# Batch 1's third split into fetch, rows and gate steps, with scaling and copies on ScalarE

## The chip, the cores and the metric

The kernel runs on one core of one Trainium2 chip. The metric is the device time of one execution in microseconds, lower is better. Engines are named as in the profile: PE is TensorE (PEld its weight loads), DVE is VectorE, ACT is ScalarE, POOL is GpSimd, SP is SyncE, which issues most DMA transfers. A queue's DMA issues are marked SPq, ACTq and POOLq.

## The reference

Three layers follow one another on 4 batches of 3072 tokens with 256 channels:

```
X  = rfft(x, axis=1)                       # spectral layer
Y  = shrink(X @ (w_r + i w_i) + b, 0.01)   # real and imaginary part each
y  = irfft(Y)                              # 12288 tokens x 256
logits = y @ w_gate; e = argmax; gate = softmax(logits)[e]
disp[e, pos] = y[i] for the first 384 tokens of each of 8 experts
h  = relu(disp @ w1[e]) @ w2[e];  out[i] = gate[i] * h[e, pos]
g  = out @ w_in;  result = (g * sigmoid(g)) @ w_out
```

At most 8 x 384 tokens go through an expert; all other rows of the result are zero.

## The kernel before

Every matrix product in reduced precision is made of three matmuls over a high and a low part of both operands (`mm3`, lines 208 to 210). High parts are cast by ACT (`hi`, line 192), low parts are differences made by DVE or POOL (`lo`, line 200). The order of instructions on each engine is set by a scheduler when the program is built: it takes the program in the order in which the generators are stepped, keeps dependencies, and places each instruction by a model of time. `after` adds an order for this scheduler only; on the chip it is no wait. Each DMA signals one of eight semaphores in turn, and a DMA that takes a semaphore waits until the earlier DMA on it has landed.

`near` computes batch 0 and the spectra of batch 1 (written to `b_d`). Tokens of batch 0 are routed, and the first experts, sorted so that those that batch 0 fills come first, can begin. `experts` then runs the order 0, 1, 2, E, 3, 4, E+1, 5, 6, E+2, 7, E+3, where a number is an expert's first layer (`first_ffn`) and E the second one for a pair of experts (`second_ffn`).

`first_ffn` makes 8 blocks j: six matmuls into a PSUM tile `hp` (operands `xT` and `w` of line 1066's loads), a relu by ACT into `hh`, the low part `hl` by DVE, and six matmuls into two accumulators `y`. It yields 9 times. At the end the two accumulators are copied to `yf`, one by ACT (line 1130), one by DVE (line 1131); only then can the next expert write its own. `weights` loads an expert's weights in four quarters through four buffers `st` of 256 KB; each load waits until the split of an earlier one has read its buffer. `turn` scales the gathered rows `xg` of the next expert by their gate (line 1095, three pieces on DVE), transposes them on PE (`gtp`) and splits them into `xT`. `pair` makes the operands `ms` and `yT` of the second layer by sums of two experts' `yf`.

Beside experts 0 to 2 runs `third(1)`: the last part of batch 1's inverse transform for a third of its tokens, with their logits, in four steps n. `rows(n)` fetches 768 KB of `b_d` in two DMAs on SP's queue (tiles `br`, `bi`, `by`; line 587), makes eight matmuls (line 590), copies to `ao` (ACT) and writes `attn` in four DMAs; `gate(n)` transposes `ao` on PE (`tp`), copies to `aT` on DVE (line 606) and makes the logits (`lg`); every second one is followed by a transpose `lt` and by `choose`, a chain of small DVE operations with an Exp on ACT. `rows(n)` and `gate(n-1)` stand in one step. Then `route` turns choices into places: a scan, the sums `bs` on PE, a chain on DVE up to `pm`, eight matmuls `tb`, and `slots`.

`beside` yields the count at which it wants to be stepped next, in blocks j over all experts: 7, then 8, 10, 12, 14 and 16, so the steps fall into experts 0 and 1.

Of the kernel before, what the change touches and what calls it, by code (L numbers as in the profile page):

```python
# [9 lines left out]
F32 = mybir.dt.float32  # L10
FR = mybir.dt.float32r
I32 = mybir.dt.int32
ALU = mybir.AluOpType
AF = mybir.ActivationFunctionType
# [5 lines left out]
Q = 96  # L20
# [3 lines left out]
P = 128  # L24
LAM = 0.01
NT = B * S
QB, GT = 32, 8
# [13 lines left out]
RING = 2  # L41
LATE = 3
PACE = {4: 2, 5: 5, **{n: GT - 1 for n in range(6, 12)}}
HOLD = {10: "lt", 14: "bs", 18: "tb"}
BIG = 65536.0
UP = 65536.0
# [109 lines left out]
class Kernel:  # L156
# [202 lines left out]
    CH = 512  # L359
# [209 lines left out]
    def third(self, b, res):  # L569

        nc, bp, ps, wg, CH = self.nc, self.bp, self.ps, self.wg, self.CH
        v = nc.vector
        c4 = self.c4[:Q, 64:]
        bv = self.bds[b].rearrange("k (r u g) c -> (k r) u (g c)", r=4, u=4)
        od = self.attn[0][b * S:b * S + QB * TW].rearrange("(q u g) d -> u q (g d)", u=4, g=GT)
        res[b] = self.chosen(1)
        idle = self.mg.tile([P, 3, 2, CH], F32, tag="ms", name="bi", bufs=1)
        room = {n + 2: idle[:Q, n] for n in range(3)}
        room[5] = self.mh.tile([P, 2, CH], F32, tag="yT", name="by", bufs=1)[:Q]

        def rows(n):
            pt = ps.tile([P, CH], F32, tag="ps", name="ps2")
            for w in range(2):
                br = room.get(2 * n + w)
                if br is None:
                    br = bp.tile([Q, 2, CH], F32, tag="xt", name="br", bufs=self.sb)
                nc.sync.dma_start(out=br, in_=bv[:, 2 * w:2 * w + 2, n * CH:(n + 1) * CH])
                for z in range(2):
                    u = 2 * w + z
                    ins = nc.tensor.matmul(pt[u * QB:(u + 1) * QB], c4, br[:, z], start=True, stop=True).ins  # L590
                    if b == 1 and not u:
                        self.after(ins, self.lasty)
            ao = bp.tile([P, 2, 2, P], F32, tag="ao", name="ao2")
            aof = ao.rearrange("p g h d -> p (g h d)")
            nc.scalar.copy(aof, pt)
            for u in range(4):
                nc.sync.dma_start(out=od[u, :, n * CH:(n + 1) * CH], in_=aof[u * QB:(u + 1) * QB])
            return ao

        def gate(n, ao):  # L600
            tp = ps.tile([P, 2, 2, P], F32, tag="ps", name="tp")
            for g in range(2):
                for h in range(2):
                    nc.tensor.transpose(tp[:, g, h], ao[:, g, h], self.ident)
            aT = bp.tile([P, 2, 2, P], F32, tag="aT", name="aT", bufs=1)
            v.tensor_copy(aT, tp)
            if n % 2 == 0:
                self.lg = ps.tile([P, P], F32, tag="ps", name="lg")
            for h in range(2):
                for g in range(2):  # L610
                    at = COL * (2 * (n % 2) + g)
                    nc.tensor.matmul(self.lg[at:at + COL], wg[:, h], aT[:, g, h], start=h == 0, stop=h == 1)
            if n % 2:
                ls = bp.tile([P, P], F32, tag="ls", name="ls", bufs=1)
                nc.scalar.copy(ls, self.lg)
                lt = ps.tile([P, 4, COL], F32, tag="ps", name="lt")
                nc.tensor.transpose(lt.rearrange("p g e -> p (g e)"), ls, self.ident)
                self.choose(lt.rearrange("p (o g) e -> p o g e", o=1)[:, :, :, :E], res[b], slice(2 * n - 2, 2 * n + 2))

        ao = {}  # L620
        for n in range(GT // 2 + 1):
            if n < GT // 2:
                ao[n] = rows(n)
            if n:
                gate(n - 1, ao.pop(n - 1))
            yield

    def is2(self, b, qbs, res):
# [320 lines left out]
    def experts(self, again=False):  # L949
        tc = self.tc  # L950
        tag = "b" if again else "a"
# [6 lines left out]
        ps = dict(space=bass.MemoryType.PSUM)  # L958
# [10 lines left out]
        def beside():  # L969

            with self.stream("b", 2, "left"):
                yield 7
                for n, _ in enumerate(self.third(1, self.res)):
                    yield 8 + 2 * n
                tiny = self.mc.tile([P, 1], F32, name="tiny")
                self.route(1, (0,), self.res)
                self.sl.extend(self.slots(self.mc, EARLY, E, self.sel, "t")[0])
                self.after(self.nc.scalar.activation(tiny, self.zt[:, 0, :1], AF.Silu).ins, self.exps)
                self.filled()
                zeros()  # L980
            self.po, self.mb = pool("po", **ps), pool("mb")
# [22 lines left out]
        n = 0  # L1004
# [87 lines left out]
    def turn(self, rows, behind=None):  # L1092
        xg, gw = rows
        for j in range(SC):
            ins = self.nc.vector.tensor_scalar(xg[:, j], xg[:, j], gw[:, j:j + 1], None, ALU.mult)
            if behind:
                self.after(ins.ins, behind)
        xT = self.mx.tile([P, 2, 2, CAP], FR, tag="xT", name="xT")
# [7 lines left out]
    def first_ffn(self, e, xT, ws):  # L1106
# [21 lines left out]
            yield  # L1128
        y = self.ys[e] = self.mg.tile([P, 2, CAP], F32, tag="yf", name="yf", bufs=3)
        nc.scalar.copy(y[:, 0], yp[0])  # L1130
        nc.vector.tensor_copy(y[:, 1], yp[1])

    def pair(self, behind=None):

# [256 lines left out]
```

## Time and profile before

| what | us |
|---|---|
| median of 3 runs | 616.54 (615.39 to 617.16) |
| the profiled execution | 617.55 |
| its span, first to last instruction | 615.8 |
| PE busy in the span | 593.4 |
| DVE busy | 424.7 |
| ACT busy | 339.3 |
| POOL busy | 187.0 |

A span is the time between the first and the last instruction of the profiled execution; the execution's own time is 1.75 us longer. An engine's busy time says what it did, not what limited the kernel. Rows in order of time give the start, the length, the engine with the line of the program, the operation, the tile written and the tile read, the shape, a count, and in brackets the idle time before it with the instruction that ended it. The granted clock of TensorE is 1.00 at 2.4 GHz and 0.50 at 1.2 GHz.

### The profile page before, as it was taken

Reading aid. Unit: us, or ns where it says so; the run is one execution under the profiler, and the core shown is the slowest. Engines: PE = TensorE matmul, PEld = TensorE weight load, DVE = VectorE, ACT = ScalarE, POOL = GpSimd, SP = SyncE. Lnnn points to the kernel's source line nnn. Section 1 sums busy time; section 2 is a strip of 40 time slices with the busy share of each in tenths; the row PEclk is TensorE's granted clock in tenths of the full one; section 3 lists DMA queues with packets and bytes.
Section 4 is the critical chain, followed back from the end, with each engine's and each line's share of the span. In section 5 each row is a group of like instructions: output and inputs, shape, how many; then the busy total and the mean of one; then the engine's idle time right before and its main releaser. Section 6 shows DMA issues by size and latency. Waiting matters only on the chain. (4 is left out here: it accounts for less than half of the span.)

```text
span 615.8 us, 11426 instructions
## 1 busy us (share of the span) xinstructions
PE 593.4 (96%) x4104; PEld 556.1 (90%) x4104; DVE 424.7 (69%) x844; ACT 339.3 (55%) x723; POOL 187.0 (30%) x189
## 2 busy tenths in 40 slices
PE   9999999999989799899999999999999999999994
PEld 9887799667988589789999999999999999989994
DVE  2468765449977589998876786587587577486563
ACT  2546554336525465556765756655567556365562
POOL 1001110002053023177453505435403442154433
PEclk9999999999999799989999999999999999999998
DMA  8829775996357976433633532404433230010001
GB/s 223 254 78 277 249 219 168 250 278 180 105 183 209 248 226 191 143 120 99 197 120 116 169 125 97 155 23 138 150 113 106 91 100 26 0 65 27 16 2 56
DMA packets 65755, 86.09 MB, mean 140 GB/s; under 512 B 5812, under 2 KB 55608, under 8 KB 65688
## 3 DMA queue, kind: packets, MB, share of 16 engines
q1 hardware_dynamic: 53720, 69.53, 37.8%
q10 hardware_dynamic: 9664, 9.44, 5.2%
q0 software_dynamic: 2304, 6.29, 3.2%
q8 instruction: 34, 0.56, 0.4%
q14 instruction: 33, 0.27, 0.2%
HBM read 54.31 MB, written 30.93 MB: 138 GB/s over the span
## 5 line engine op out<-in xcount | busy, mean ns | idle before, releaser
L1289 DVE TENSOR_TENSOR u<-h,u 128x384 f32<-128x384 f32 x224 | 117.9, 552 | 59.9 <-PE h L210 51.6
L1199 ACT ACTIVATE u<-u 128x384 f32<-128x384 f32 x128 | 64.6, 522 | 73.1 <-DVE u L1289 71.1
L209 PE MATMUL o<-wo,gl 128*128 128x256 f32 x354 | 94.5, 280 | 0.9 <-DVE gl L200 0.9
L210 PE MATMUL o<-wo,gh 128*128 128x256 f32 x354 | 94.6, 280 | 0.0
L208 PE MATMUL o<-wo,gh 128*128 128x256 f32 x354 | 83.1, 280 | 0.0
L200 POOL TENSOR_TENSOR ring<-mt,ring 128x384 fp32r<-128x384 f32 x32 | 38.0, 1190 | 136.3 <-ACT ring L192 136.3
L200 POOL TENSOR_TENSOR gl<-u,gh 128x384 fp32r<-128x384 f32 x62 | 64.8, 1060 | 29.6 <-ACT gh L192 29.5
L209 PEld LDWEIGHTS o<-wo,gl 128*128 128x128 f32 x354 | 66.5, 188 | 1.2 <-DVE gl L200 1.2
L210 PEld LDWEIGHTS o<-wo,gh 128*128 128x128 f32 x354 | 66.5, 188 | 0.0
L192 ACT CAST gh<-u 128x384 fp32r<-128x384 f32 x126 | 63.1, 509 | 5.7 <-PE o L210 4.0
L208 PEld LDWEIGHTS o<-wo,gh 128*128 128x128 f32 x354 | 62.4, 188 | 0.0
L208 PE MATMUL yp<-wri,xk 128*128 128x256 f32 x188 | 56.1, 298 | 0.0
L210 PE MATMUL yp<-wri,xk 128*128 128x256 f32 x188 | 54.0, 287 | 0.0
L209 PE MATMUL yp<-wri,xk 128*128 128x256 f32 x188 | 53.7, 286 | 0.0
L192 ACT CAST w<-st 128x512 fp32r<-128x512 f32 x64 | 38.6, 619 | 23.5 <-DMA st<-in_moe_w 15.7
L200 DVE TENSOR_TENSOR w<-st,w 128x512 fp32r<-128x512 f32 x56 | 39.6, 717 | 17.1 <-ACT w L192 12.0
L1120 ACT ACTIVATE hh<-hp 128x384 fp32r<-128x384 f32 x64 | 31.1, 489 | 35.4 <-PE y L209 13.7
L1121 DVE SCALAR_TENSOR_TENSOR hl<-hp,hh 128x384 fp32r<-128x384 f32 x64 | 34.9, 552 | 21.6 <-ACT hh L1120 16.3
L200 POOL TENSOR_TENSOR wi<-na,wi 128x256 fp32r<-128x256 f32 (+1 forms) x8 | 8.1, 1012 | 132.9 <-ACT wi L192 132.9
L208 PE MATMUL hp<-xT,w 128*128 128x384 f32 x128 | 43.8, 343 | 4.2 <-ACT w L192 4.1
L200 DVE TENSOR_TENSOR gl<-u,gh 128x384 fp32r<-128x384 f32 x64 | 42.8, 669 | 2.2 <-ACT gh L192 2.1
L208 PE MATMUL y<-hh,w 128*128 128x384 f32 x128 | 43.7, 341 | 0.5 <-ACT hh L1120 0.5
(254 smaller groups left out, 1543.1 us busy)
## 6 DMA issues: line engine op xcount, KB each, us to landing
st<-in_moe_w SPq DMA_DIRECT2D x64, 256.0 KB, 2.9
out<-zt SPq DMA_DIRECT2D x48, 256.0 KB, 3.5
b_d<-bo ACTq DMA_DIRECT2D x12, 512.0 KB, 3.1
mt<-mixed SPq DMA_DIRECT2D x32, 192.0 KB, 2.3
xt<-in_x SPq DMA_DIRECT2D x15, 384.0 KB, 6.7
nt<-in_moe_w_in SPq DMA_DIRECT2D x8, 512.0 KB
nt<-in_moe_w_out SPq DMA_DIRECT2D x16, 256.0 KB, 3.0
a_d<-ao SPq DMA_DIRECT2D x8, 384.0 KB, 3.4
```

Of the source, the lines that this page charges most:

```text
L192: self.lastact = self.nc.scalar.copy(dst, src)
L200: return e.tensor_tensor(dst, src, raw(hi), ALU.subtract).ins
L208: first = nc.tensor.matmul(out, lh, rh, start=start, stop=False)
L209: nc.tensor.matmul(out, ll, rh, start=False, stop=False)
L210: return first.ins, nc.tensor.matmul(out, lh, rl, start=False, stop=stop).ins
L1120: self.rectified = nc.scalar.activation(hh, hp, AF.Relu).ins
L1121: self.evicted = nc.vector.scalar_tensor_tensor(hl, hp, 0.0, raw(hh), ALU.max, ALU.subtract).ins
L1199: act.activation(sg, sg, AF.Silu)
L1289: v.tensor_tensor(to, h, u, ALU.add)
```

## The change

The third of batch 1 is split into 12 steps: fetch (f), rows (r) and gate (g), each of 0 to 3, in the order f0 f1 r0 f2 g0 r1 f3 g1 r2 g2 r3 g3. They are due at the counts 5, 6, 7, 8, 8, 9, 10, 10, 11, 12, 12 and 13, and the route at 13. Fetch 0 is issued by SP, the others by ACT; each is placed after the last y matmul so far, for the scheduler only. Three kinds of work move from DVE to ACT: the scaling in `turn` (three per expert), the copy of `aT` (four in all), and the copy of the second accumulator at an expert's end.

```diff
--- before.py
+++ after.py
@@ -41,6 +41,8 @@
 RING = 2
 LATE = 3
 PACE = {4: 2, 5: 5, **{n: GT - 1 for n in range(6, 12)}}
+STEPS = *zip("ffrfgrfgrgrg", (0, 1, 0, 2, 0, 1, 3, 1, 2, 2, 3, 3)),
+DUE = 5, 6, 7, 8, 8, 9, 10, 10, 11, 12, 12, 13, 13
 HOLD = {10: "lt", 14: "bs", 18: "tb"}
 BIG = 65536.0
 UP = 65536.0
@@ -578,18 +580,20 @@
         room = {n + 2: idle[:Q, n] for n in range(3)}
         room[5] = self.mh.tile([P, 2, CH], F32, tag="yT", name="by", bufs=1)[:Q]
 
-        def rows(n):
-            pt = ps.tile([P, CH], F32, tag="ps", name="ps2")
+        def fetch(n):
             for w in range(2):
                 br = room.get(2 * n + w)
                 if br is None:
-                    br = bp.tile([Q, 2, CH], F32, tag="xt", name="br", bufs=self.sb)
-                nc.sync.dma_start(out=br, in_=bv[:, 2 * w:2 * w + 2, n * CH:(n + 1) * CH])
-                for z in range(2):
-                    u = 2 * w + z
-                    ins = nc.tensor.matmul(pt[u * QB:(u + 1) * QB], c4, br[:, z], start=True, stop=True).ins
-                    if b == 1 and not u:
-                        self.after(ins, self.lasty)
+                    br = room[2 * n + w] = bp.tile([Q, 2, CH], F32, tag="xt", name="br", bufs=self.sb)
+                ins = (nc.scalar if n else nc.sync).dma_start(out=br, in_=bv[:, 2 * w:2 * w + 2, n * CH:(n + 1) * CH])
+                self.after(ins.ins, self.lasty)
+
+        def rows(n):
+            pt = ps.tile([P, CH], F32, tag="ps", name="ps2")
+            for u in range(4):
+                ins = nc.tensor.matmul(pt[u * QB:(u + 1) * QB], c4, room[2 * n + u // 2][:, u % 2], start=True, stop=True).ins
+                if not u:
+                    self.after(ins, self.lasty)
             ao = bp.tile([P, 2, 2, P], F32, tag="ao", name="ao2")
             aof = ao.rearrange("p g h d -> p (g h d)")
             nc.scalar.copy(aof, pt)
@@ -603,7 +607,7 @@
                 for h in range(2):
                     nc.tensor.transpose(tp[:, g, h], ao[:, g, h], self.ident)
             aT = bp.tile([P, 2, 2, P], F32, tag="aT", name="aT", bufs=1)
-            v.tensor_copy(aT, tp)
+            nc.scalar.copy(aT, tp)
             if n % 2 == 0:
                 self.lg = ps.tile([P, P], F32, tag="ps", name="lg")
             for h in range(2):
@@ -618,11 +622,13 @@
                 self.choose(lt.rearrange("p (o g) e -> p o g e", o=1)[:, :, :, :E], res[b], slice(2 * n - 2, 2 * n + 2))
 
         ao = {}
-        for n in range(GT // 2 + 1):
-            if n < GT // 2:
+        for kind, n in STEPS:
+            if kind == "f":
+                fetch(n)
+            elif kind == "r":
                 ao[n] = rows(n)
-            if n:
-                gate(n - 1, ao.pop(n - 1))
+            else:
+                gate(n, ao.pop(n))
             yield
 
     def is2(self, b, qbs, res):
@@ -969,9 +975,9 @@
         def beside():
 
             with self.stream("b", 2, "left"):
-                yield 7
+                yield DUE[0]
                 for n, _ in enumerate(self.third(1, self.res)):
-                    yield 8 + 2 * n
+                    yield DUE[n + 1]
                 tiny = self.mc.tile([P, 1], F32, name="tiny")
                 self.route(1, (0,), self.res)
                 self.sl.extend(self.slots(self.mc, EARLY, E, self.sel, "t")[0])
@@ -1092,7 +1098,7 @@
     def turn(self, rows, behind=None):
         xg, gw = rows
         for j in range(SC):
-            ins = self.nc.vector.tensor_scalar(xg[:, j], xg[:, j], gw[:, j:j + 1], None, ALU.mult)
+            ins = self.nc.scalar.activation(xg[:, j], xg[:, j], AF.Copy, scale=gw[:, j:j + 1])
             if behind:
                 self.after(ins.ins, behind)
         xT = self.mx.tile([P, 2, 2, CAP], FR, tag="xT", name="xT")
@@ -1128,7 +1134,7 @@
             yield
         y = self.ys[e] = self.mg.tile([P, 2, CAP], F32, tag="yf", name="yf", bufs=3)
         nc.scalar.copy(y[:, 0], yp[0])
-        nc.vector.tensor_copy(y[:, 1], yp[1])
+        nc.scalar.copy(y[:, 1], yp[1])
 
     def pair(self, behind=None):
```

The order that the scheduler makes of it differs at three places that matter below.

SP's queue, late in expert 0. Before (`st_2316` and `st_2321` are the last quarter of expert 0's weights; `br`, `bi`, `by` are fetches of the third; ISA rows only compute addresses):

```order
L1066 ISA
L1066 DMA st_2285<-in_moe_w2 128x2x256 [waits DMAHW7_49,DVE_49]
L587 DMA br_2386<-b_d1_1049 96x2x512 [waits DMAHW4_49,DMAHW2_49,PE_49]
L587 DMA br_2390<-b_d1_1049 96x2x512
L587 DMA bi_2383<-b_d1_1049 96x2x512 [waits DMAHW0_49,PE_49]
L1066 ISA
L1066 DMA st_2316<-in_moe_w1 128x2x256 [waits DMAHW1_49,DVE_49]
L1066 ISA
L1066 DMA st_2321<-in_moe_w2 128x2x256 [waits DVE_49]
L587 DMA bi_2383<-b_d1_1049 96x2x512 [waits DMAHW3_49]
L587 DMA bi_2383<-b_d1_1049 96x2x512
L587 DMA by_2384<-b_d1_1049 96x2x512 [waits DMAHW5_49]
```

With the change (here `st_2352` and `st_2357` are expert 1's second quarter):

```order
L1072 ISA
L1072 DMA st_2285<-in_moe_w2 128x2x256 [waits DMAHW7_49,DVE_49]
L1072 ISA
L1072 DMA st_2316<-in_moe_w1 128x2x256 [waits DMAHW0_49,DVE_49]
L1072 ISA
L1072 DMA st_2321<-in_moe_w2 128x2x256 [waits DMAHW1_49,DVE_49]
L588 DMA br_2331<-b_d1_1049 96x2x512 [waits DMAHW4_49,DMAHW2_49,PE_49]
L588 DMA br_2333<-b_d1_1049 96x2x512
L1072 ISA
L1072 DMA st_2352<-in_moe_w1 128x2x256 [waits DMAHW3_49,DVE_49]
L1072 ISA
L1072 DMA st_2357<-in_moe_w2 128x2x256 [waits DMAHW5_49,Pool_49]
```

The two loads of expert 0's last quarter now stand ahead of all fetches, and of six fetches in a row two are left on this queue.

ACT, from the end of expert 0 into expert 1. Before (`ao2_2394` is the copy of rows 0, `xT` expert 1's input, the `w` expert 1's weights):

```order
L1120 ACTIVATE hh_2333<-hp_2326 128x384 [waits DVE_49,PE_49]
L192 CAST w0_2318<-st_2316 128x512 [waits DMAHW1_49]
L192 CAST wo_2106<-na_2290 128x512 [waits DVE_49]
L192 CAST w1_2323<-st_2321 128x512 [waits DMAHW2_49,PE_49]
L595 COPY ao2_2394<-ps2_2385 128x512 [waits PE_49]
L192 CAST xT_2412<-gtp_2413 128x384 [waits PE_49]
L192 CAST xT_2412<-gtp_2419 128x384 [waits PE_49]
L1120 ACTIVATE hh_2360<-hp_2353 128x384 [waits PE_49,Activation_49]
L192 CAST w0_2345<-st_2343 128x512 [waits DMAHW6_49]
L192 CAST w1_2350<-st_2348 128x512 [waits DMAHW7_49]
L1120 ACTIVATE hh_2432<-hp_2425 128x384 [waits DVE_49,PE_49]
```

With the change, from the first operation behind `xT` (`bi_2329` and `by_2330` are fetch 2, `br_2564` and `br_2566` fetch 3; `yf_2488` is the copy that frees an accumulator for expert 1's first `y`):

```order
L588 DMA bi_2329<-b_d1_1049 96x2x512 [waits DMAHW1_49]
L588 DMA by_2330<-b_d1_1049 96x2x512
L194 CAST w0_2383<-st_2381 128x512 [waits DMAHW6_49,DVE_49,PE_49]
L1126 ACTIVATE hh_2434<-hp_2427 128x384 [waits DVE_49]
L610 COPY aT_2461<-tp_2456 128x512 [waits PE_49]
L194 CAST wo_2106<-na_2402 128x512 [waits DVE_49]
L1126 ACTIVATE hh_2560<-hp_2553 128x384 [waits PE_49,Activation_49]
L588 DMA br_2564<-b_d1_1049 96x2x512 [waits DMAHW1_49,DMAHW0_49]
L588 DMA br_2566<-b_d1_1049 96x2x512 [waits DMAHW3_49]
L194 CAST w0_2446<-st_2444 128x512 [waits DMAHW0_49,PE_49]
L1126 ACTIVATE hh_2601<-hp_2594 128x384 [waits DVE_49,PE_49]
L1136 COPY yf_2488<-y0_2186 128x384 [waits PE_49]
```

Four DMA issues now stand among ACT's casts and relus. The two of fetch 3 wait on the semaphores DMAHW1 and DMAHW3, which the two of fetch 2 signal when they have landed; `hh_2601` and `yf_2488` stand behind them.

PE, at the end of expert 2 (`y_2904` and `y_2905` its accumulators, `tb` the route's last matmuls, `h_3138` a product of the second layer). Before, where 31 matmuls stand between `bs` and `tb`:

```order
L208 MATMUL y_2904<-hh,w_2546 128x384
L209 MATMUL y_2904<-hh,w_2546 128x384
L208 MATMUL y_2905<-hh,w_2546 128x384
L209 MATMUL y_2905<-hh,w_2546 128x384
L768 MATMUL tb<-ft,pm 128x72 x8
L210 MATMUL y_2904<-hl,w_2546 128x384
L210 MATMUL y_2905<-hl,w_2546 128x384
L208 MATMUL h_3138<-ms,wi 128x384
L209 MATMUL h_3138<-ms,wi 128x384
```

With the change, from the second `bs` on:

```order
L719 MATMUL bs<-inc,rt 128x8
L212 MATMUL y_2904<-hl,w_2548 128x384
L212 MATMUL y_2905<-hl,w_2548 128x384
L210 MATMUL y_2904<-hh,w_2548 128x384
L211 MATMUL y_2904<-hh,w_2548 128x384
L210 MATMUL y_2905<-hh,w_2548 128x384
L211 MATMUL y_2905<-hh,w_2548 128x384
L212 MATMUL y_2904<-hl,w_2548 128x384
L212 MATMUL y_2905<-hl,w_2548 128x384
L774 MATMUL tb<-ft,pm 128x72 x8
L210 MATMUL h_3138<-ms,wi 128x384
```

Eight matmuls are left between `bs` and `tb`, and all of expert 2's stand ahead of `tb`. The matmuls of rows 3 (`ps2`) have moved from the middle of expert 1 to behind expert 2's first `hp`.

## Rows read from the trace of the kernel before

**Rows 1.** The page's first part: busy time of each engine.

```profile
PE 593.4 (96%) x4104; PEld 556.1 (90%) x4104; DVE 424.7 (69%) x844; ACT 339.3 (55%) x723; POOL 187.0 (30%) x189
```

**Rows 2.** Busy time by stretch: PE, PEld, DVE, ACT, POOL, granted clock, DMA share, GB/s.

```profile
200.00:205.00 5.00, 0.89 (x4) 0.57 (x3) 1.71 (x6) 1.06 (x2) 0.00 (x0) 0.95 1.09 236
205.00:210.00 5.00, 5.00 (x20) 2.90 (x20) 1.96 (x4) 2.14 (x5) 0.00 (x0) 0.50 1.08 257
210.00:215.00 5.00, 5.00 (x29) 4.13 (x28) 3.78 (x8) 2.95 (x6) 1.29 (x1) 0.87 0.93 249
260.00:265.00 5.00, 3.45 (x12) 3.13 (x13) 4.90 (x16) 1.80 (x5) 3.20 (x2) 0.75 0.02 3
265.00:270.00 5.00, 4.78 (x22) 3.81 (x21) 4.22 (x8) 3.57 (x9) 4.12 (x4) 0.91 0.68 213
450.00:500.00 50.00, 50.00 (x338) 49.63 (x337) 34.63 (x66) 30.40 (x67) 15.98 (x15) 1.00 0.35 112
```

**Rows 3.** PE in order of time, experts 0 and 1: start, us, what.

```profile
204.61 0.69 PE L208 MATMUL hp<-xT,w 128*128 128x384 f32 x1 [4.11 <-ACT w L192]
214.22 1.07 PE L590 MATMUL ps<-bi,c 96*32 96x512 f32 x8
215.22 0.66 PE L604 MATMUL tp<-ident,ao 128*128 128x128 f32 x4
217.80 0.33 PE L208 MATMUL hp<-xT,w 128*128 128x384 f32 x1
219.71 0.34 PE L210 MATMUL hp<-xT,w 128*128 128x384 f32 x1
233.75 0.82 PE L1102 MATMUL gtp<-ident,xg 128*128 128x128 f32 x6
```

**Rows 4.** SP's queue in order of time.

```profile
194.18 0.84 SPq L587 DMA_DIRECT2D br<-b_d  x2
195.12 0.39 SPq L587 DMA_DIRECT2D bi<-b_d  x1
195.76 0.40 SPq L1066 DMA_DIRECT2D st<-in_moe_w  x1
```

**Rows 5.** DMA issues from three stretches (195.5, 207 and 220 us): count, size, us to landing.

```profile
st<-in_moe_w SPq DMA_DIRECT2D x1, 256.0 KB, 8.2
br<-b_d SPq DMA_DIRECT2D x1, 384.0 KB, 7.2
st<-in_moe_w SPq DMA_DIRECT2D x1, 256.0 KB, 2.9
```

**Rows 6.** DVE (first two) and ACT in order of time, expert 0.

```profile
193.57 1.29 DVE L200 TENSOR_TENSOR w<-st,w 128x512 fp32r<-128x512 f32 x2
199.03 0.68 DVE L900 SCALAR_TENSOR_TENSOR na<-nt,na 128x512 int32<-128x512 int32 x1
203.94 0.62 ACT L192 CAST w<-st 128x512 fp32r<-128x512 f32 x1 [5.88 <-DMA st<-in_moe_w]
204.46 0.61 ACT L192 CAST wo<-na 128x512 fp32r<-128x512 f32 x1
```

**Rows 7.** PE in order of time, end of expert 2.

```profile
257.73 0.98 PE L768 MATMUL tb<-ft,pm 128*128 128x72 f32 x8
260.40 0.44 PE L208 MATMUL h<-ms,wi 128*128 128x384 f32 x1 [1.22 <-ACT ms L192]
262.17 0.45 PE L210 MATMUL h<-ms,wi 128*128 128x384 f32 x1 [1.15 <-DVE ms L200]
```

**Rows 8.** DVE's scalings by tile xg after 270; ACT's order of time (last two).

```profile
L1095 DVE TENSOR_SCALAR xg<-xg,gwt x15: 341/347/1110, 307.3 to 506.4; 128x256 f32<-128x256 f32 x15
170.64 0.41 ACT L462 ACTIVATE xk<-xk 128x256 fp32r<-128x256 f32 x1
189.96 0.37 ACTq L497 DMA_DIRECT2D b_d<-bo  x1
```

**Rows 9.** DVE in order of time, end of expert 2.

```profile
252.42 0.23 DVE L714 TENSOR_TENSOR inc<-inc,oh 128x64 f32<-128x64 f32 x1
260.53 0.55 DVE L1131 COPY yf<-y 128x384 f32<-128x384 f32 x1
```

## The prediction

> **What bounds the kernel now.** I read the page's first part, then busy time by stretch, then TensorE's own order of time, and last the DMA queue and the two copy engines around each gap. TensorE (PE) is busy 593.4 of 615.8 us [rows 1]. From about 270 us on it has no gap: a late stretch shows 50.00 of 50.00 busy at full clock [rows 2]. So the change can gain only where PE stands still, and that is in two places, both of which it touches.
>
> The first is late in expert 0. PE stops for 4.11 us until 204.61, for the last quarter of expert 0's first weights [rows 3]. The granted clock is then 0.50 from 205 to 210 and 0.87 from 210 to 215 (1.2 instead of 2.4 GHz for most of it) while PE is busy throughout [rows 2]: 5 x 0.50 + 5 x 0.13 = 3.2 us of work lost, and some 0.1 before 205. The place costs 7.4 us. Its cause stands in SP's queue: three fetches of 384 KB were issued from 194.18 on, and the two weight loads only from 195.76 [rows 4]; the first of these landed 8.2 us after its issue, where a load in a quiet stretch takes 2.9 [rows 5]. ScalarE casts it at 203.94 and does nothing for 5.88 us before; the next cast in its order, of wo, waits behind it although VectorE had finished its input at 199.7 [rows 6]. ScalarE works strictly in order, which matters below.
>
> The second is the end of expert 2, where the pair of experts 0 and 1 must be ready: PE stands for 1.22 us before 260.40 and 1.15 us before 262.17 [rows 7], 2.4 us together, and the clock falls to a mean of 0.75 [rows 2].
>
> **The change part by part.** *The fetches leave the weights' way.* In the new SP order expert 0's last quarter stands ahead of all fetches. Its first load needs the buffer whose split VectorE ends at about 194.3 (the first of the two from 193.57) [rows 6], so it is issued at about 194.3 and lands in 3 to 4 us, before PE wants it at 200.5. PE's work from there to the first turn of the third (tp) is 20 matmuls at 0.174 us (11 steps in 1.91 us [rows 3]), eight of rows (1.07 [rows 3]) and six transposes (0.82 [rows 3]): 5.4 us, so 205.9. Before, tp came at 215.22, but six hp and eight rows matmuls that now follow it (2.1 us) were done by then; like for like 213.1. That is the whole 7.4 us. What gives some of it back:
>
> (a) Fetch 0's second half now ends 1.31 MB (two loads, two fetches) from 194.3. Before, 1.44 MB from 194.18 took until 203.94, 9.8 us [rows 4, 6]; in proportion 8.9, so 203.2. PE comes to those rows at 201.9: **1.3 us**.
>
> (b) Expert 1's second quarter lies behind that: 1.57 MB, 10.6 us, 204.9. ScalarE's next cast waits for it, and behind this cast stands the hh that PE needs after its transposes, at 204.6; 204.9 + 0.62 (cast) + 0.5 is 206.0: **1.4 us**. Against this order the Trainium skill, "Trainium Kernel Development and Optimization", section Key Constraints, has a rule: queues of SP, ScalarE and POOL run on the same 16 DMA engines and interleave, so another queue saves only issue time. DMA was already full (share 1.09 at 200 to 205 [rows 2]); the two fetches that ScalarE issues at about 199.5 would by this rule go in among the weights; the price of that is a rival's below, and no run here yet shows it.
>
> (c) The copy of rows 0 stands behind the next weight cast (0.62 [rows 6]), and xT behind the copy: **0.9 us** by the length of such copies.
>
> (d) Half clock after these gaps: 2.4 us of gap before 262 was followed by a loss of some 1.7 us (5 x 0.25 + 5 x 0.09 [rows 2]); the new gaps are as long but in more pieces, so half: **0.8 us**.
>
> (e) *Fetch 3 on ScalarE.* Both its issues wait for fetch 2's landing (the same semaphores), which ScalarE issued only five operations and, at their lengths of 0.5 to 0.6, some 2.7 us earlier; behind it stand an hh and the copy of y0 that frees PE's next accumulator. After the landing ScalarE needs 0.7 (two issues at 0.37 [rows 8]) + 0.6 + 0.5 + 0.5 = 2.3; PE has 5.8 us of its own work (18 hp, 6 y's, lg and rows). With a landing time L, PE stands L - 2.7 + 2.3 - 5.8 = L - 6.2. L lies between 2.9 and 7.2 [rows 5]; I take 7.0, near the row of the same transfer: **0.8 us** (0 to 1.0, more if DMA is fuller).
>
> (f) *The end of expert 2.* The table of counts moves the route from 16 to 13, but the order as built does not follow it: rows 3 stand behind expert 2's first hp, and the route's first sums (bs) have moved from 31 matmuls ahead of tb to 8. VectorE's chain from bs to the last ms that PE needs runs from 252.42 to 262.17 [rows 7, 9], 9.75 us; two hl and a yf copy of about 0.47 each leave it, 8.35. PE has only 8 x 0.174 + 0.9 (tb) + 0.35 = 2.65 of its own in it, so stands 5.7 instead of 2.4: **3.3 us** more. The half clock after it should stay about what it was, since it lasts from the gap until PE has been busy again, as before.
>
> *Moved work.* Of 24 scalings VectorE gives up 0.35 each [rows 8] and ScalarE takes about 0.41 (nearest row, the same 128x256 shape [rows 8]); with 4 aT copies (0.62, as a cast of that shape [rows 6]), 8 yf copies (0.55 on VectorE [rows 9]) and 6 issues ScalarE goes from 339 to about 358 us, 58% of the span, VectorE from 425 to 409. In expert 1 ScalarE comes near full. After 270 us this is covered by PE's own unbroken work; if that cover is gone, each scaled turn could cost PE up to 3 x 0.41 = 1.2 us, five times. I count nothing. Removing VectorE's scaling gains nothing either: PE waits there for data, not for VectorE's length. At expert 0's start the third gather decides, not the engine that scales.
>
> Sum: -7.4 + 1.3 + 1.4 + 0.9 + 0.8 + 0.8 + 3.3 = +1.1 us. The profiled execution took 617.55, so 618.7 for such a one; the median of the runs is 616.54, 1.0 below it, so **617.6** for the median. That is no change that can be measured: about 0.3%, 1.85 us, is what a measurement of this kernel can tell.
>
> **The rivals.** *The transfers are not the limit* (faster): the loads move in the order written and fetch 0 lands within 5 us of its issue. Then (a) to (e) shrink to some 1.0 us and (f) stays: -7.4 + 1.0 + 3.3 = -3.1, **613.4**. For it: a quiet load lands in 2.9 us, and the time of 8.2 includes imbalance that a shorter queue has less of. Against: a DMA share of 1 and more up to 215 [rows 2].
>
> *Fetches among the weights* (slower): in 200 to 205 fetch 1 takes turns with expert 1's second quarter. As much again as that load (0.26 MB at 0.148 MB per us, 1.8 us) goes in front of it; hh comes at 207.8 and PE stands 3.2 us in (b): **619.4**. It decides as soon as ScalarE's fetches begin before that load is through. By the rule named in (b) this is what happens; the rows show only that DMA was full with one queue.
>
> *ScalarE held before fetch 3* (slower than before): this is (e) grown large. Place: expert 1's first y. It hurts from L = 6.2 us and makes the kernel measurably slower from about L = 7.8; a landing after 9.5 us, as when loads, four attn writes and weights of expert 2 are still queued, costs 3.3 us, 2.5 more than taken: **620.1**. For it: 7.2 and 8.2 us have been seen [rows 5]. Against: DMA is less full after 215.
>
> **How the numbers follow.** Forecast 0.37, by itself 615 to 618.4; faster 0.28; fetches among the weights 0.20; ScalarE held 0.15. So faster 0.28, same 0.37, slower 0.35. The range goes from 613.0, just below the faster case, to 621.5, where both slower cases meet in part; what is left out is all waits falling away, or clock losses on top of both.
>
> **What would show it.** Right: no 4 us wait for expert 0's weights; small waits for rows, hh and ao between 200 and 212; PE idle before expert 1's first y with ScalarE's DMA issue ahead; before tb and the first ms some 5.7 us of idle; a granted clock of half after it. Wrong: expert 1 begins late by another wait, PE passes tb without a gap, or gaps after 270 us.

## The result and the profile after

The changed kernel took **624.11 us** (623.12 to 626.01, four runs) against 616.85 for the kernel before beside it (615.39 to 619.18): ratio 1.0122, 95% interval 1.0100 to 1.0145. It is slower by some 7.3 us; 617.6 was predicted, with a range up to 621.5. The profiled execution took 624.13, with a span of 622.3. All line numbers below are those of the changed kernel, two to six higher than before.

The first part of its page (busy time, share, instructions) answers to [rows 1]:

```profile
PE 596.2 (96%) x4104; PEld 556.0 (89%) x4104; DVE 402.9 (65%) x808; ACT 353.7 (57%) x759; POOL 183.0 (29%) x189
```

VectorE gave up 21.8 us and ScalarE took 14.4, and TensorE's busy time rose by 2.8 with the same number of instructions. The stretches of the changed kernel (columns as in [rows 2]):

```profile
200.00:205.00 5.00, 4.30 (x26) 2.76 (x25) 2.92 (x6) 2.11 (x5) 0.00 (x0) 1.00 1.09 238
205.00:210.00 5.00, 3.44 (x19) 2.75 (x18) 2.69 (x7) 3.10 (x7) 1.27 (x1) 1.00 1.01 260
210.00:215.00 5.00, 5.00 (x35) 3.46 (x35) 2.86 (x7) 2.42 (x7) 0.00 (x0) 1.00 0.94 283
220.00:225.00 5.00, 2.99 (x15) 2.02 (x15) 3.31 (x5) 3.13 (x7) 1.27 (x1) 0.75 0.63 204
225.00:230.00 5.00, 5.00 (x32) 4.29 (x30) 4.05 (x7) 3.23 (x7) 1.85 (x2) 0.91 0.49 163
255.00:260.00 5.00, 2.22 (x16) 1.92 (x14) 4.49 (x20) 1.75 (x4) 0.00 (x0) 1.00 0.01 2
260.00:265.00 5.00, 3.83 (x14) 3.19 (x15) 4.96 (x14) 2.83 (x6) 1.21 (x1) 0.51 0.00 0
265.00:270.00 5.00, 4.65 (x21) 3.84 (x19) 4.25 (x12) 2.10 (x5) 4.08 (x5) 0.81 0.55 174
350.00:355.00 5.00, 2.46 (x13) 1.88 (x12) 1.71 (x4) 2.31 (x5) 2.90 (x3) 1.00 0.50 155
355.00:360.00 5.00, 4.76 (x19) 4.43 (x17) 5.00 (x11) 4.44 (x10) 0.00 (x0) 0.66 0.19 61
```

The 4 us wait at 200 to 205 is gone: PE is busy 4.30 of 5 where it was 0.89 [rows 2]. In its place there are three stretches with a gap and a clock of 0.51 to 0.75 behind it, at 220, at 255 to 265 and at 350 to 360. In the last of them the kernel before had no gap at all:

```profile
350.00:355.00 5.00, 5.00 (x29) 4.76 (x28) 5.00 (x11) 3.63 (x8) 0.00 (x0) 1.00 0.45 136
355.00:360.00 5.00, 5.00 (x31) 5.00 (x30) 3.59 (x7) 2.09 (x5) 0.00 (x0) 1.00 0.39 129
```

PE in order of time shows the heads of the gaps, and at 216.35 expert 1's first y, which has none:

```profile
204.34 0.45 PE L210 MATMUL y<-hh,w 128*128 128x384 f32 x1 [0.49 <-ACT hh L1126]
208.06 0.65 PE L608 MATMUL tp<-ident,ao 128*128 128x128 f32 x4 [1.24 <-ACT ao L599]
216.35 0.33 PE L210 MATMUL y<-hh,w 128*128 128x384 f32 x1
222.10 0.44 PE L210 MATMUL y<-hh,w 128*128 128x384 f32 x1 [2.01 <-ACT hh L1126]
259.86 1.71 PE L774 MATMUL tb<-ft,pm 128*128 128x72 f32 x8 [2.78 <-DVE pm L762]
262.19 0.69 PE L210 MATMUL h<-ms,wi 128*128 128x384 f32 x1 [0.62 <-ACT ms L194]
263.75 0.69 PE L212 MATMUL h<-ms,wi 128*128 128x384 f32 x1 [0.55 <-DVE ms L202]
354.10 0.44 PE L210 MATMUL y<-hh,w 128*128 128x384 f32 x1 [2.34 <-issue]
360.38 0.62 PE L212 MATMUL y<-hl,w 128*128 128x384 f32 x2 [0.61 <-DVE hl L1127]
```

By the order as built the y at 222.10 belongs to expert 1's third block j, two blocks behind its first y.

To see where time is lost for good I put the same product of PE side by side: the h products, counted in order, start in both traces in the same sequence. Against the first profile of before, the first h stands at -1.7 us, the 34th (270.23 before) at +1.6, the 166th (322.14) still at +1.6, the 199th (368.81) at +7.0, the 364th (466.80) at +7.4 and the last at +6.55. I call this the ladder. So the change gained 1.7 us up to expert 2's end, lost 3.3 there, and lost 5.4 between 350 and 361 us, at expert 4's first y: 3.2 us of gaps, 1.7 of half clock (5 x 0.34) and some in pieces.

What ScalarE did there, in order of time: an hh, a cast and an hh, each 1 to 2.2 us after what the order makes them wait for had ended, as far as the trace shows.

```profile
346.27 0.48 ACT L1126 ACTIVATE hh<-hp 128x384 fp32r<-128x384 f32 x1
349.28 0.49 ACT L1126 ACTIVATE hh<-hp 128x384 fp32r<-128x384 f32 x1 [2.52 <-PE y L212]
350.73 0.62 ACT L194 CAST w<-st 128x512 fp32r<-128x512 f32 x1 [0.96 <-remote]
352.84 0.49 ACT L1126 ACTIVATE hh<-hp 128x384 fp32r<-128x384 f32 x1 [1.49 <-DVE w L202]
353.56 0.48 ACT L1136 COPY yf<-y 128x384 f32<-128x384 f32 x1 [0.23 <-remote]
```

The copy of y at 353.56 frees the accumulator of expert 4's first y, which starts at 354.10. By the order as built the hh of 349.28 needs only the hp that PE ended near 347.1.

### The profile page after: what moved, and what is told of

It reads as the page before. It is cut to its first block, busy times and chain, and to the rows that moved or that the text cites. A ratio compares the mean times of both kernels' runs of the same rounds, so it can differ in the third digit from the quotient of the medians.

```text
span 622.3 us, 11433 instructions
## 1 busy us (share of the span) xinstructions
PE 596.2 (96%) x4104; PEld 556.0 (89%) x4104; DVE 402.9 (65%) x808; ACT 353.7 (57%) x759; POOL 183.0 (29%) x189
## 5 line engine op out<-in xcount | busy, mean ns | idle before, releaser
L202 POOL TENSOR_TENSOR gl<-u,gh 128x384 fp32r<-128x384 f32 x62 | 63.5, 1041 | 37.7 <-ACT gh L194 36.8
L210 PE MATMUL hp<-xT,w 128*128 128x384 f32 x128 | 44.0, 345 | 0.6 <-DVE xT L202 0.3
L211 PE MATMUL hp<-xT,w 128*128 128x384 f32 x128 | 43.5, 340 | 0.6 <-DVE w L202 0.6
```

What stands on the lines that cost most here:

```text
L202: return e.tensor_tensor(dst, src, raw(hi), ALU.subtract).ins
L210: first = nc.tensor.matmul(out, lh, rh, start=start, stop=False)
L211: nc.tensor.matmul(out, ll, rh, start=False, stop=False)
```

## Experiments

Each run gives a median, its ratio to the kernel before run beside it (not the quotient of the two medians), and two gaps of PE in its profile: ahead of tb (end of expert 2), and ahead of expert 4's first y with the hl behind it. "bs" is how many matmuls stand between bs and tb in PE's order as built; where expectations below speak of 42 and 26, the order as built and the traces have 40 and 33.

| run | us (before) | ratio, 95% | bs | at tb | at expert 4 |
|---|---|---|---|---|---|
| changed kernel | 624.11 (616.85) | 1.0122, 1.0100-1.0145 | 8 | 2.78 | 2.34 + 0.61 |
| scale_on_dve | 619.54 (615.49) | 1.0081, 1.0051-1.0110 | 22 | 0.70 | 0.23 |
| y1_on_dve | 621.19 (615.49) | 1.0086, 1.0059-1.0113 | 8 | 3.35 | none |
| split_alone | 619.54 (615.49) | 1.0073, 1.0048-1.0098 | 8 | 3.36 | none |
| copies_alone | 617.86 (615.49) | 1.0040, 1.0019-1.0060 | 36 | none | 0.23 |
| after_again | 620.37 (616.09) | 1.0067, 1.0048-1.0086 | 8 | 2.79 | 0.23 |
| pad_16 | 618.84 (616.09) | 1.0050, 1.0025-1.0075 | 8 | 2.77 | 0.23 |
| pad_64 | 620.52 (616.09) | 1.0071, 1.0047-1.0095 | 8 | 2.78 | 0.23 |
| before_again | 616.87 (616.09) | 1.0024, 1.0001-1.0046 | 31 | none | none |
| rows_first | 619.11 (615.87) | 1.0039, 1.0018-1.0060 | 40 | none | 2.00 + 0.62 |
| fetch_on_sp | 626.21 (615.87) | 1.0148, 1.0117-1.0180 | 8 | 2.78 | 2.75 + 0.22 |
| rows_first_dve | 614.96 (615.87) | 0.9973, 0.9950-0.9997 | 33 | none | none |
| rows_first_dve_sp | 615.11 (615.87) | 0.9981, 0.9956-1.0005 | 33 | none | none |
| sp_again | 625.16 (616.19) | 1.0138, 1.0107-1.0169 | 8 | 2.79 | 2.41 + 1.22 |
| sp_pad_16 | 625.49 (616.19) | 1.0148, 1.0108-1.0188 | 8 | 2.78 | 2.39 + 1.18 |
| sp_pad_128 | 622.77 (616.19) | 1.0122, 1.0094-1.0150 | 8 | 2.77 | 2.89 |
| rows_first_dve_again | 615.19 (616.19) | 1.0001, 0.9976-1.0027 | 33 | none | none |
| sp_scale_on_dve | 624.70 (617.05) | 1.0121, 1.0086-1.0156 | 8 | 2.78 | 0.23 |
| sp_y1_on_dve | 623.51 (617.05) | 1.0120, 1.0084-1.0155 | 8 | 3.36 | 1.69 + 1.23 |

before_again is the kernel before against itself, and its interval (1.0001 to 1.0046) still leaves out 1: a difference of a quarter of a per cent can be chance here.

### Undoing one part, or doing one alone

**scale_on_dve**: the changed kernel, with

```diff
-            ins = self.nc.scalar.activation(xg[:, j], xg[:, j], AF.Copy, scale=gw[:, j:j + 1])
+            ins = self.nc.vector.tensor_scalar(xg[:, j], xg[:, j], gw[:, j:j + 1], None, ALU.mult)
```

> The changed kernel with the scaling of xg back on VectorE, all else as changed. In the changed kernel PE stands 2.34 us ahead of expert 4's first y (354.10) and 0.61 us at 360.38, with a clock of about one half between (some 5 us in all against the kernel before). Theory A (the scaling on ScalarE stands ahead of the copies of tail in its queue, so the six scatters of the output run in one piece from 342 to 349.5 us and the three gathers after them to 353.5, and ScalarE's and VectorE's steps of expert 4 are late beside them): the gap goes, 619 us (618 to 620.5). Theory B (the second copy of y on ScalarE makes the first y late): the gap stays, 623.5 to 625. Theory C (ScalarE's own instructions arrive late at a place that depends on how many it has executed): the gap goes or moves, 618 to 624, and it goes in every kernel with another count of ScalarE's instructions.

**y1_on_dve**: the changed kernel, with

```diff
-        nc.scalar.copy(y[:, 1], yp[1])
+        nc.vector.tensor_copy(y[:, 1], yp[1])
```

> The changed kernel with the copy of y's second half back on VectorE, all else as changed (the scaling stays on ScalarE). Theory A: the scatters still run in one piece behind the scaling, the gap of 2.3 us ahead of expert 4's first y stays, 623 to 625 us. Theory B: the gap goes, 619 us (618 to 620.5). Theory C: the gap goes or moves (three instructions fewer on ScalarE up to there), 618 to 624.

**split_alone**: both of these edits and

```diff
-            nc.scalar.copy(aT, tp)
+            v.tensor_copy(aT, tp)
```

> The kernel before with the third step of batch 1 split alone (fetch, rows and gate by the new order, fetches 1 to 3 on ScalarE); scaling, aT and both copies as before. The ladder of the changed kernel puts +1.6 us on all up to 264 us. Theories A, B and C alike: PE has no gap from 270 to 550 us, 617 to 619.5 us; the two gaps ahead of 264 us (about 2.0 us at expert 1's first y, about 2.8 us ahead of tb) stay. If the split is what makes the late gap, 623 to 625.

**copies_alone**: the kernel before, with the first two edits the other way round (scaling and y's second half on ScalarE).

> The kernel before with the scaling and the second copy of y on ScalarE alone; the third step of batch 1 as before. Theories A and B: a gap of 2 to 3 us ahead of expert 4's first y with half clock behind it, and the 4.1 us wait for the weights at 204.6 us as before: 620 to 623 us. Theory C: the gap stands elsewhere or not at all, 616 to 619 us.

All four lack the late gap, copies_alone too, which has the scaling and the copies on ScalarE and the six scatters in one piece. As the next runs show, that says little, since the unedited kernel can lack it as well; A, B and C stay open. The split alone costs 0.7%, most of the loss. Its ladder goes from -1.9 us at the first h to +1.8 at the 34th: the end of expert 2 again. (Of the two early gaps that were expected to stay, only the one at tb did; there is none at 222 us, but 2.24 us ahead of tp at 206.42.) scale_on_dve points at what decides at the end of expert 2. With bs 22 matmuls ahead of tb instead of 8, its gap at tb shrinks to a quarter, while the two waits for ms behind it grow to 1.27 and 0.94 us:

```profile
257.69 1.06 PE L774 MATMUL tb<-ft,pm 128*128 128x72 f32 x8 [0.70 <-DVE pm L762]
```

A second, small cost came to light. Every kernel with both copies of y on ScalarE has a row like this at the first turn of a pair (longer with the late gap, and sp_pad_128 has the late gap in its place) and another a hundred us later. The two rows here, of scale_on_dve at 353.08 and 452.06, add 0.4 to 0.5 us each to the ladder; y1_on_dve, split_alone and both profiles of before have neither:

```profile
353.08 0.61 PE L212 MATMUL y<-hl,w 128*128 128x384 f32 x2 [0.23 <-DVE hl L1127]
```

### The same kernels again, and ScalarE's count of instructions

**after_again** and **before_again** have no edit. **pad_16** and **pad_64** are the changed kernel with (64 in the second)

```diff
         nc.vector.memset(self.zt, 0.0)
+        pad = cst.tile([P, 1], F32, name="pad")
+        for _ in range(16):
+            nc.scalar.copy(pad, self.zt[:, 0, :1])
```

> The changed kernel once more, nothing edited. If the late gap belongs to the kernel (its order and its number of instructions), PE stands again over 2 us ahead of expert 4's first y and the time is 623 to 626 us. If it was a stall of that execution, the gap is gone in this profile and the time is 619 to 621 us.

> The kernel before once more, nothing edited. Its runs spread from 613.8 to 617.5 us, and the profile that the prediction used lies at the top of them. All theories: no gap from 270 to 550 us. If the spread comes from the waits for transfers in expert 0, the waits between 195 and 270 us differ from the first profile by as much as the two times do.

> The changed kernel with 16 copies of one element per partition ahead of everything on ScalarE; the order of all engines behind them is unchanged. Theory C (ScalarE's instructions arrive late at a place set by their count): the place moves by 16 instructions of ScalarE, the gap ahead of expert 4's first y goes or moves to another place, 618 to 624 us. If the order or the data set it: the same gap at expert 4's first y, 623.5 to 626 us.

> The same with 64 such copies. Theory C: no gap at expert 4's first y, 618 to 624 us and another place than with 16. If the order or the data set it: the same gap, 623.5 to 626 us. The copies run while nothing else does at the start and are expected to cost under 1 us themselves; if they hold up the first loads, up to 6 us more by the first rows and not by the late gap.

The unedited kernel had no late gap this time. ScalarE in after_again, the same five instructions, each within 0.6 us of what it needs:

```profile
348.95 0.48 ACT L1126 ACTIVATE hh<-hp 128x384 fp32r<-128x384 f32 x1
349.81 0.49 ACT L1126 ACTIVATE hh<-hp 128x384 fp32r<-128x384 f32 x1 [0.38 <-PE hp L212]
350.85 0.62 ACT L194 CAST w<-st 128x512 fp32r<-128x512 f32 x1 [0.55 <-PE hp L212]
351.54 0.49 ACT L1126 ACTIVATE hh<-hp 128x384 fp32r<-128x384 f32 x1
351.93 0.47 ACT L1136 COPY yf<-y 128x384 f32<-128x384 f32 x1
```

So the change costs some 4.3 us (ratio 1.0067) without the gap, and the first record's 7.3 has the gap in it. The gap's 5.4 us do not simply add to the 4.3: the stretch up to the 34th h also varies, +1.6 us on the ladder in the first profile and +3.9 in after_again. That the two padded kernels lack it proves nothing, since the unpadded one lacked it beside them. before_again shows why the first profile of before was a dear one: its wait for expert 0's weights was 4.11 us [rows 3], here it is shorter, and the ladder stands at -1.2 by the 34th h.

```profile
203.05 0.69 PE L208 MATMUL hp<-xT,w 128*128 128x384 f32 x1 [2.65 <-ACT w L192]
```

### The sequence of the steps, and who issues the fetches

**rows_first**: the changed kernel with the sequence that the kernel before had, rows of the next step ahead of the gate.

```diff
-STEPS = *zip("ffrfgrfgrgrg", (0, 1, 0, 2, 0, 1, 3, 1, 2, 2, 3, 3)),
+STEPS = *zip("ffrfrgfrgrgg", (0, 1, 0, 2, 1, 0, 3, 2, 1, 3, 2, 3)),
```

> The changed kernel with the twelve steps in another sequence: rows 0, rows 1, gate 0, rows 2, gate 1, rows 3, gate 2, gate 3, as in the kernel before; fetches, scaling and copies as changed. In PE's order bs then stands 42 matmuls ahead of tb (8 in the changed kernel, 22 in the one with the scaling on VectorE, 31 before). Theory F (the end of expert 2 is late because rows 3 and gate 3 stand late in PE's order, and that is the larger part of the loss): no gap ahead of tb, no half clock behind it, 3 to 4 us less than the changed kernel: 617 us (616 to 618). Theory E (the larger part is lost around expert 1's first y, where ScalarE waits for DMAs): the gap ahead of tb may go, but the wait comes back elsewhere ahead of 270 us: 619.5 to 621.

**fetch_on_sp**: the changed kernel with

```diff
-                ins = (nc.scalar if n else nc.sync).dma_start(out=br, in_=bv[:, 2 * w:2 * w + 2, n * CH:(n + 1) * CH])
+                ins = nc.sync.dma_start(out=br, in_=bv[:, 2 * w:2 * w + 2, n * CH:(n + 1) * CH])
```

> The changed kernel with all fetches issued by SP, none by ScalarE. Theory E as the prediction put it (ScalarE is held at fetch 3's issue, and PE stands ahead of expert 1's first y for that): the two gaps around expert 1 (1.0 us behind the copy of y at 216, 2.0 to 3.2 us behind hh at 223) go, 2 to 4 us less than the changed kernel: 616.5 to 618.5. Rival (ScalarE waits there for the transfers of nt and of the weights themselves, whichever engine issues the fetch): the gap at 223 stays at 2 us or more, 619.5 to 621.5. The gap ahead of tb stays in both (bs 8 matmuls ahead of tb).

**rows_first_dve**: split_alone with the sequence of rows_first. **rows_first_dve_sp**: the same with the edit of fetch_on_sp and DUE = 5, 6, 7, 8, 8, 8, 9, 10, 10, 11, 11, 12, 12.

> The kernel before with the third step split and its fetches 1 to 3 on ScalarE, in the sequence of rows_first; scaling, aT and copies on VectorE as before. bs stands 26 matmuls ahead of tb. Theory F: the first wait for the weights (2.6 to 4.1 us before) is gone, nothing at tb, no cost at the boundaries of the pairs: 615 us (613.5 to 616.5), at or under the kernel before. Theory E: 617.5 to 619.5.

> The same with all fetches issued by SP and the later steps due one earlier; bs 26 matmuls ahead of tb. Theory F without E: as rows_first_dve, 613.5 to 616.5. If ScalarE's issue of fetch 3 costs what the prediction put (0.8 us) or more, 1 to 3 us less than rows_first_dve. If SP's queue of weights is held by the fetches' waits for a lane, 1 to 3 us more.

Theory F holds. With rows ahead of gates PE passes tb without a gap and at full clock (rows_first; its next wait is short):

```profile
253.32 0.98 PE L774 MATMUL tb<-ft,pm 128*128 128x72 f32 x8
257.88 0.44 PE L210 MATMUL h<-ms,wi 128*128 128x384 f32 x1 [0.56 <-ACT yf L1136]
```

Its ladder is at -4.9 us by the 34th h where the changed kernel has +1.6. Of this 1.5 us go again by the 166th, where a wait of 1.13 us stands ahead of an o at 267.19, so 5.0 us are won there. The late gap, in this profile, takes 4.6 back; without it the time would be below the 616 to 618 us that were expected. With scaling and copies on VectorE as well, rows_first_dve has neither loss and comes out level with the kernel before.

fetch_on_sp settles what holds PE at expert 1's third block (222.10 in the changed kernel). The gap stays though ScalarE issues no fetch:

```profile
220.74 0.44 PE L210 MATMUL y<-hh,w 128*128 128x384 f32 x1 [2.07 <-ACT hh L1126]
```

So it was not fetch 3's issue. ScalarE in the changed kernel, in order of time (the ACTq row is that issue), waits at 219.15 and 221.04 for transfers of wo's rows (nt) and of the weights (st), and the hh that PE needs stands behind them:

```profile
206.90 0.62 ACT L194 CAST w<-st 128x512 fp32r<-128x512 f32 x1 [2.62 <-DMA st<-in_moe_w]
211.88 1.68 ACTq L588 DMA_DIRECT2D br<-b_d  x2
213.66 0.62 ACT L194 CAST w<-st 128x512 fp32r<-128x512 f32 x1 [2.58 <-DMA nt<-in_moe_w_out]
219.15 0.68 ACT L899 ACTIVATE na<-nt 128x512 f32<-128x512 f32 x1 [2.72 <-DMA nt<-in_moe_w_out]
221.04 0.62 ACT L194 CAST w<-st 128x512 fp32r<-128x512 f32 x1 [1.20 <-DMA st<-in_moe_w]
221.56 0.48 ACT L1126 ACTIVATE hh<-hp 128x384 fp32r<-128x384 f32 x1
```

The one wait of 5.88 us before [rows 6] has become several of 1.2 to 2.7, spread over two experts. The one at 213.66 is another matter: the cast stands right behind fetch 3's two issues, the second of which starts at 213.25, so ScalarE was held there for fetch 2's landing, as the prediction said, whatever releaser the row names. In this profile that cost PE nothing (216.35). In four others of the ten with fetches on ScalarE, PE waits at expert 1's first y for the copy behind these issues: 1.00 us in pad_16, 0.85 in pad_64, and (after_again, y1_on_dve)

```profile
216.59 0.44 PE L210 MATMUL y<-hh,w 128*128 128x384 f32 x1 [1.05 <-ACT yf L1136]
219.22 0.69 PE L210 MATMUL y<-hh,w 128*128 128x384 f32 x1 [2.41 <-ACT yf L1136]
```

In none of the seven profiles with all fetches on SP does PE wait there. So theory E holds for its first gap and falls for the second.

The Trainium skill ("Trainium Kernel Development and Optimization", Key Constraints) says that queues of different engines share the DMA engines, so that a second queue saves issue time alone; rows_first_dve and rows_first_dve_sp, 614.96 and 615.11 us beside each other (the second also has its later steps due one earlier), agree with it.

### The late gap

fetch_on_sp had the late gap and took over 623 us in all its runs, so the next five start from it. **sp_again** has no edit; **sp_pad_16** and **sp_pad_128** have the copies of pad_16 (16 and 128 of them); **sp_scale_on_dve** and **sp_y1_on_dve** have the edits of scale_on_dve and y1_on_dve.

> The kernel with all fetches on SP once more, nothing edited; its six runs took 623.2 to 627.9 us and its profile has the late gap (2.75 us ahead of expert 4's first y, ladder +5.4 us there). If the late gap belongs to the program, it stands again: 623 to 628 us. If it comes and goes with something outside the program (the changed kernel showed it in one profile of two), 617 to 622 us without it.

> The same with 16 one-element copies ahead on ScalarE; no other order changes. Theory C (ScalarE's own instructions arrive late where its block of them ends; in the changed kernel the packet of the second instruction queue came at 352.4 us, with 16 copies ahead at 338.4, so it is ScalarE's): no gap ahead of expert 4's first y, about 5 us less than the kernel without the copies, 617 to 621 us. If the gap has another cause in the order or the data: as without the copies, 623 to 628 us.

> The same with 128 such copies: one packet of the second instruction queue holds 8 KB, which at 64 B for one would be 128 instructions (an estimate: 34 packets, 0.28 MB), so the end of a block falls on the same place as without copies. Order unchanged on all engines from 50 us on. Theory C: the packet near 352 us and the late gap are there again, as in the kernel without copies, plus up to 8 us from the copies themselves in the first 25 us, by the first rows. If copies ahead merely shift things: no gap.

> The kernel with all fetches on SP, whose four profiles (with and without copies ahead) all show the late gap, now with the scaling back on VectorE; both copies of y stay on ScalarE. On ScalarE the copies of tail are then no longer behind the scaling, and the scatters go out two and four, not six in one piece ahead of the gathers. Theory A2 (ScalarE's waits of 1 to 3 us come up only beside the unbroken series of six scatters and three gathers on POOL): no late gap, 617.5 to 620.5 us. Theory B (both copies of y on ScalarE): gap stays, 622 to 627 us.

> The same kernel with the second copy of y back on VectorE; the scaling stays on ScalarE, so the six scatters and three gathers are one series. Theory A2: the late gap stays, 621 to 626 us. Theory B: no gap, 617 to 620 us. If neither this nor sp_scale_on_dve shows the gap, the chip or the occasion decides it and the cause stays open.

Theory C falls: the gap stands at the same y with 0, 16 and 128 instructions more. Theory B falls: with y's second half on VectorE it is still there (sp_y1_on_dve),

```profile
352.25 0.45 PE L210 MATMUL y<-hh,w 128*128 128x384 f32 x1 [1.69 <-issue]
357.60 0.62 PE L212 MATMUL y<-hl,w 128*128 128x384 f32 x2 [1.23 <-DVE hl L1127]
```

and it goes with the scaling on VectorE. On ScalarE the scaling stands ahead of the copies of tail, so POOL gets its six scatters at once and runs them and the three gathers behind them as one series (sp_y1_on_dve, POOL in order of time; first and last scatter, first gather):

```profile
341.37 1.03 POOL L1343 DMA_INDIRECT out<-tail,dsts  x1 [10.38 <-ACT tail L1246]
347.88 0.98 POOL L1343 DMA_INDIRECT out<-tail,dsts  x1 [0.31 <-issue]
349.17 1.05 POOL L1090 DMA_INDIRECT xg<-attn,srct  x1 [0.30 <-issue]
```

With the scaling on VectorE two scatters go first and POOL rests for 4 us (sp_scale_on_dve):

```profile
341.73 1.03 POOL L1343 DMA_INDIRECT out<-tail,dsts  x1 [3.79 <-ACT tail L1246]
343.07 1.00 POOL L1343 DMA_INDIRECT out<-tail,dsts  x1 [0.31 <-issue]
348.10 1.34 POOL L1343 DMA_INDIRECT out<-tail,dsts  x1 [4.03 <-ACT tail L1246]
```

Over all profiles, the gap shows in 7 of 12 with the scaling on ScalarE and in none of 8 with it on VectorE. The 12 divide by the chip that the record names: none of five on two chips (numbers 11 and 15), all six on three others (1, 6 and 7), and the first record, which names none. On those three chips four profiles with the scaling on VectorE have no gap. So in these profiles the gap does not come without the scaling on ScalarE, and that alone is not enough. What else decides is not settled: all six on the three chips have the fetches on SP or the sequence of rows_first, and only the changed kernel itself was seen both with the gap (first record) and without it (chip 11), so the chip, the occasion and, for the others, the program stand together. That the unbroken series on POOL is the link is argued from its place, not shown: the series is unbroken in the five without the gap too, and no run breaks the series and leaves the scaling on ScalarE. sp_scale_on_dve shows also that losing the late gap does not make this kernel fast, and it misses the time expected of it: its ladder is at +8.2 us by the 34th h, with PE waits of 2.16 us at 222.86, 1.33 at 237.58, 1.61 at 251.36 and 2.78 ahead of tb.

**rows_first_dve_again** is rows_first_dve once more.

> The version that came out lowest (614.96 against 615.87 us, ratio 0.9973 with 0.995 to 0.9997) once more, nothing edited, to see whether it is below the kernel before on another occasion: 0.995 to 1.000. If the first was chance: 1.000 to 1.004.

The first result was chance: 0.9973 and 1.0001 together say the same as the kernel before. No version of these beats it.

## Why the prediction was wrong

The total was 617.6; measured are 624.1 with the late gap and 620.4 without. Step by step, by the first profile:

- *The first wait goes*: right; no wait of 4 us is left. The wait was also priced at its dearest, 4.11 us; on another occasion it was 2.65.
- *(a) rows 0 wait for fetch 0, 1.3*: no such gap in this trace (0.32 and 0.73 in y1_on_dve). *(b) hh, 1.4*: 0.49 us at 204.34. *(c) ao and xT, 0.9*: 1.24 at 208.06 and 0.32 at 209.03.
- *(d) half clock after these, 0.8*: none; the clock is 1.00 from 200 to 215.
- *(e) fetch 3 on ScalarE, 0.8*: nothing in this trace, though ScalarE was held there for 2.58 us. Fetch 2's second half was issued at 207.34 and had landed by 213.25, within 5.9 us, and the term's own formula gives nothing below 6.2. The mechanism is right: in the four profiles with a gap at this place the landing took 8.1 to 9.7 us and PE waited 0.85 to 2.41, where the formula gives 1.9 to 3.5. In rows_first, another order, the landing took as long and PE did not wait.
- *What no term had*: PE stood 2.01 us at 222.10, in expert 1's third block, for ScalarE's waits for nt and st, and half clock took 1.7 more (5 x 0.25 + 5 x 0.09). So (a) to (e), 5.2 in all, came out as 2.1, and with these 3.7 as 5.8. That the ladder says -1.7 us where the steps gave -2.2 is luck.
- *(f) the end of expert 2, 3.3*: right in place and cause; the ladder goes from -1.7 to +1.6, and rows_first, which only moves rows 1 to 3 ahead of gates 0 to 2, takes the gap away. The size is partly luck. PE's gaps there are 4.3 us (2.78, 0.62, 0.55 and 0.30), not 5.7, but the half clock, which was to stay as it was, grew from 1.7 us to 3.4 (5 x 0.49 + 5 x 0.19).
- *Moved work, "I count nothing"*: **the step that failed.** The ladder goes from +1.6 to +6.55 after 270 us. Of this 5.4 us lie at expert 4's first y and 0.4 at the second turn of a pair, and 0.8 us come back at the last pair. The prediction looked at the scaling's length, where ScalarE has room, and at what waits for it, which does come in time. What the runs show in its place is the late gap, which comes in 7 of 12 profiles with the scaling on ScalarE and in none of 8 without. The prediction did not follow what the scaling stands ahead of in ScalarE's queue: the copies of tail, and behind them POOL's scatters and gathers. That this is how the scaling makes the gap is argued, not shown. The price that it set aside for lost cover, 1.2 us a turn, was too small for this place and too large for the others.

Of the rivals, fetches among the weights put 3.2 us at the hh of (b), where 0.49 came. ScalarE held before fetch 3 came at its place in four later profiles, with 0.85 to 2.41 us for landings of 8.1 to 9.7 where it gave 3.3 for 9.5, and not in the first. What the prediction named as a sign of being wrong, gaps after 270 us, is what came.

Without the late gap the loss is placed by the mean ladder of after_again, pad_16 and pad_64 against that of the two profiles of before: -1.0 us at the first h, +2.5 at the 34th, +2.8 at the 166th, +4.4 at the last, beside 4.3 measured for after_again (2.8 and 4.4 for the padded ones). So 3.5 us are lost at the end of expert 2 and 1.6 after 322 us: some 0.9 at two turns of a pair, and the rest at the last pair, where PE waits 1.5 us ahead of an o (0.91 and 0.42 in the two profiles of before). That last part is not firm: against the first profile of before alone it is 0.2. Why that wait is longer was not tried.

## What to carry over

When an instruction moves to another engine, follow what stands behind it in the new queue, through every engine that this feeds, and not only its length and its own consumer; "PE has no gaps there" is no cover if the queue behind feeds the next stage. When a step is cut into pieces, check where the last piece stands in the bound engine's order: here moving the rows ahead of the gates took away a gap of 2.8 us and the half clock behind it, for a wait of 1.1 us a little later. Profile the kernel before twice before pricing a wait by one trace.

## What was not expected of the hardware

ScalarE stood 1 to 3 us at a time with its inputs ready, in one short stretch beside a series of POOL's indirect DMAs, in one profile of the changed kernel and not in the next (2.52, 0.96 and 1.49 us in the first, at most 0.55 in the second). What holds it is open. The executions of an unchanged kernel also spread more than its first three told: 613.8 to 617.5 us in one set of 13 for the kernel before, and 618.5 to 623.1 in ten for the changed one.
